# A cross network on one core: group 6's output gathered in a free input slot, group 7's output in group 6's slot, and group 6's last copy and store issued one tile sooner

## The chip, the cores and the metric

The kernel runs on one core of a Trainium2 chip. The metric is the device time of one execution in microseconds. A core has TensorE (matmul), VectorE, ScalarE, GpSimd and SyncE, which run their own instruction queues side by side and wait for each other through semaphores. In the profile they are PE, DVE, ACT, POOL and SP. DMAs are issued by instructions in such a queue (here nearly all by SP, in order) and carried out by 16 DMA engines.

## The reference

A cross network over 16,384 rows of 416 features, with six layers, in bfloat16:

```python
B, F, D, L = 16384, 26, 16, 6          # Din = 26 * 16 = 416
def reference(x0, ws, bs):             # x0 (B, Din), ws (L, Din, Din), bs (L, Din)
    x = x0
    L = ws.shape[0]
    for l in range(L):
        proj = jnp.einsum('bd,de->be', x, ws[l]) + bs[l]
        x = x0 * proj + x
    return x
```

## The kernel before

The rows are cut into eight groups of 2,048 (`GC`), numbered 0 to 7; `LAST` is 7. A group is four chunks of 512 rows (`NJ`, `CH`). Features lie on the partitions: 416 are three tiles of 128 (`NT`, tiles 0 to 2) and a tail of 32. A job (g, l) is layer l of group g. For each tile it multiplies on TensorE, ScalarE takes the result out of PSUM with the bias added (`evacuate`, L519, and `evacuate_chunk`, L555), and VectorE multiplies by x0 (L528, L567) and adds x (L533, L572). The tails of several jobs are done together (`tails`).

The input of a group is kept transposed in one of five slots `x0s[0]` to `x0s[4]`; `slot(g)` is g modulo 5. A slot is loaded by DMAs that transpose. Results of a layer lie in `xs`, tails in `x3s`.

The result of layer 5 lies with features on partitions and must be written row by row. For groups 0 to 6, `turn` (L888) issues one transposing DMA per tile into the tile `ost`, `turn_tail` (L896) one for the tail into `ot3`, `spread` copies the tail from `ot3` to its columns, and `store` (L929) writes the rows to DRAM. All these DMAs are issued by SP. There is one `ost` for groups 0 to 6, so the first `turn` of a group waits until the store of the group before has landed. `ost` also serves as a buffer while groups are loaded. For groups up to 5 `spread` is on GpSimd, for group 6 on ScalarE (L920).

Group 7's last layer is done the other way round: its matmuls (L1143) make rows on the partitions at once, in four steps `kk` of 128 rows of each chunk. ScalarE takes each out into the tile `on` (L1195), VectorE multiplies it by x0 (L1201) and adds the residual x (L1207), and `nat_store` (L1214) writes it. The residual has to be turned from features on partitions to rows: `rest_turn` (L941) does that with transposing DMAs for tiles 0 and 1 of job (7, 4) into `x5n`; tile 2 is turned on TensorE and copied by VectorE (L1163), the tail by TensorE and ScalarE (L1176).

`x0n7`, `x5n` and `on` lie in input slots that are free by then: slot 3, slot 0 and slot 4.

The end of the program runs so: stream of matmuls (L1051, L1055) up to job (7, 4) tile 0; then tiles 1 and 2 of job (7, 4); after tile 0 and after tile 1 `rest_turn` is added to SP's queue, after tile 2 ScalarE's `spread` and the two halves of group 6's store; then group 7's last layer. `turn` of group 6 is added to SP's queue as each tile of job (6, 5) is finished, its last tile in two halves.

Instructions are collected by a small class `Program`: `add` takes the engine, the tokens read and written, and works out what an instruction waits for. Each engine executes its instructions in the order in which they were added; on VectorE alone an addition can be held back behind the next multiply. A DMA's `lane` is the semaphore that it counts on; DMAs of one lane and different `batch` wait for the batch before.

Of the kernel before, what the change touches and what calls it, by code (L numbers as in the profile page):

```python
# [3 lines left out]
P = 128  # L4
CH = 512
# [16 lines left out]
class Program:  # L22
# [12 lines left out]
    def add(self, eng, fn, reads=(), writes=(), lane=None, batch=None, hold=False, release=False, row=None):  # L35
        op = Op(eng, fn, lane, batch, row)
        deps = {}
        if eng == "pool":
            writes = list(writes) + ["pool"]
        for t in reads:  # L40
            w = self.writer.get(t)
            if w is not None:
                deps[id(w)] = (w, True)
        for t in writes:
            w = self.writer.get(t)
            if w is not None:
                deps[id(w)] = (w, True)
            for r in self.readers.get(t, ()):
                if id(r) not in deps:
                    deps[id(r)] = (r, False)  # L50
        for d, raw in deps.values():
            if d.lane is None and d.eng == eng and lane is None and (eng == "pe" or not raw):
                if row is None or d.row is None or row == d.row:
                    continue
            op.deps.append(d)
        for t in reads:
            self.readers.setdefault(t, []).append(op)
        for t in writes:
            self.writer[t] = op
            self.readers[t] = []  # L60
        if eng == "dve":
            if hold:
                self.flush()
                self.held = op
            else:
                self.queue[eng].append(op)
                if release:
                    self.flush()
        else:
            self.queue[eng].append(op)  # L70
        if lane is not None:
            batches = self.lanes.setdefault(lane, [])
            if not batches or batches[-1][0] != batch:
                batches.append((batch, []))
            batches[-1][1].append(op)
        return op
# [233 lines left out]
def bass_standalone__cross_network_dcn__recsys_kernel(  # L310
# [6 lines left out]
    B, D = x0.shape  # L317
    L = ws.shape[0]
    NT = 3
    NJ = 4  # L320
    GC = NJ * CH
    NG = B // GC
    KK = CH // P
    assert D == NT * P + T32 and B == NG * GC and NG == 8 and L == 6
    LAST = NG - 1
# [18 lines left out]
    XW = NT * GC  # L344
# [7 lines left out]
    x0s = [nc.alloc_sbuf_tensor(f"x0_{s}", [P, XW + 2 * CH], BF16) for s in range(NX0)]  # L352
    xs = [nc.alloc_sbuf_tensor(f"x_{s}", [P, XW], BF16) for s in range(NXS)]
# [3 lines left out]
    ost = nc.alloc_sbuf_tensor("ost", [P, GC // P, D], BF16)  # L357
    Tb = ost[:, :, :].rearrange("p a f -> p (a f)")[:, 0:GC]
    ot3 = nc.alloc_sbuf_tensor("ot3", [P, KK, P], BF16)
# [8 lines left out]
    def x0_tok(s, t, j):  # L368
        return ("x0", s, t, j)

    def x0_all(s):
        return [x0_tok(s, t, j) for t in range(NT) for j in range(NJ)] + [("x03r", s), ("x03r", s, "b")]
# [4 lines left out]
    def slot(g):  # L377
        return g % NX0
# [56 lines left out]
    def x03_toks(s):  # L435
        return [("x03q", s, j) for j in range(NJ)]
# [303 lines left out]
    def load_nat(j, k0, k1):  # L740
# [6 lines left out]
        reads=["warm"], writes=["warm"])  # L747
# [117 lines left out]
    def job_banks():  # L865
        return take(NJ)

    view = "p (j k f) -> p j k f"
    sn, so, s5 = slot(3), slot(4), slot(5)
    x0n7, x5n, on = (x0s[s][:, 0:XW + CH].rearrange(view, j=NJ, k=KK) for s in (sn, s5, so))  # L870
    rows7 = x0[LAST * GC:B, :]

    def load_last():
# [9 lines left out]
    def turn(g, t):  # L883

        s = xset[(g, L)]
        halves = ((0, 2), (2, NJ)) if (g, t) == (LAST - 1, NT - 1) else ((0, NJ),)
        for j0, j1 in halves:
            add("sp", lambda h, j0=j0, j1=j1: h.dma_start_transpose(  # L888
                ost[:, j0 * KK:j1 * KK, t * P:(t + 1) * P], xs[s][:, t * GC + j0 * CH:t * GC + j1 * CH]),
                reads=[("x", s, t, j) for j in range(j0, j1)], writes=[("ost", t, j) for j in range(j0, j1)],  # L890
                lane="ot" if g < LAST - 1 else f"ot_{t}{j0}", batch=g)

    def turn_tail(g):

        s3 = xtail[(g, L)]
        add("sp", lambda h: h.dma_start_transpose(ot3[:, :, :], x3s[s3][:, :]),  # L896
            reads=[("x3", s3)], writes=["ot3"], lane="ot3", batch=g)

    def output(g):

        s, s3 = xset[(g, L)], xtail[(g, L)]
        if g < LAST - 2:
            turn(g, 0)
        if g < LAST - 1:
            turn_tail(g)
            spread("pool")
            if g < LAST - 2:
                turn(g, 1)
                turn(g, 2)
            store(g, 0, NJ)  # L910
        free_x.append(s)
        free_3.append(s3)

    def spread(eng):

        dst = ost[:, :, NT * P:D].rearrange("p (j k) f -> p j k f", j=NJ)
        sp_ = ot3[:, :, :].rearrange("p k (j f) -> p j k f", j=NJ)
        kw = dict(reads=["ot3"], writes=[("ost", NT, j) for j in range(NJ)])
        if eng == "act":
            add("act", lambda h: h.activation(dst, sp_, ACT_F.Copy), **kw)  # L920
        else:
            add(eng, lambda h: h.tensor_copy(dst, sp_), **kw)  # L922

    def store(g, j0, j1):

        rows = out[g * GC + j0 * CH:g * GC + j1 * CH, :]
        o = ost[:, j0 * KK:j1 * KK, :].rearrange("p (j k) f -> p j k f", k=KK)
        pat = "(j p k) f -> p j k f" if g == 0 else "(j k p) f -> p j k f"
        add("sp", lambda h: h.dma_start(rows.rearrange(pat, j=j1 - j0, k=KK), o),  # L929
            reads=[("ost", t, j) for t in range(NT + 1) for j in range(j0, j1)],  # L930
            writes=[("out", g, j0)], lane="out", batch=g)

    x5f = x0s[s5][:, 0:XW + CH].rearrange("p (a f) -> p a f", f=D)
# [1 line left out]
    def rest_turn(t):  # L935

        s = xset[(LAST, L - 1)]
        if t == 0:
            add("pool", lambda h: h.memset(warm[:, :], 0.0), writes=x0_all(s5) + x03_toks(s5) + ["x5 free"])
        for j0, j1 in ((0, NJ),) if t == 0 else ((0, 2), (2, NJ)):  # L940
            add("sp", lambda h, j0=j0, j1=j1: h.dma_start_transpose(  # L941
                x5f[:, j0 * KK:j1 * KK, t * P:(t + 1) * P], xs[s][:, t * GC + j0 * CH:t * GC + j1 * CH]),
                reads=[("x", s, t, j) for j in range(j0, j1)] + ["x5 free"],
                writes=[("x5n", j, t) for j in range(j0, j1)], lane=f"x5_{t}{j0}", batch=0)
# [15 lines left out]
    k = 0  # L960
# [17 lines left out]
    def start_job(g, l, ahead=True):  # L978
        started.add((g, l))
        if ahead:  # L980
            xset[(g, l + 1)] = free_x.pop(0)
        if (g, l) in W_LOAD:
            load_wm(W_LOAD[(g, l)], "sp")
            load_w3(W_LOAD[(g, l)], "sp")
        if (g, l) in G_LOAD:
            load_group(G_LOAD[(g, l)])
# [102 lines left out]
    for n, it in enumerate(items):  # L1089
        if n == s_lo:  # L1090
            stream(items[s_lo:s_hi], NJ, 0)
        if s_lo <= n < s_hi - 1:
            continue
        if it[0] == "tails":
            tails(it[1])
            continue
        _, (g, l), i = it
        if (g, l) not in started:
            start_job(g, l)
        if n == 0:  # L1100
            two_tiles(g, l)
            continue
        if n == 1:
            continue
        if n == s_hi - 1:
            pass
        elif mode[n] in ("FR", "F1"):
            banks = job_banks()
            full(g, l, i, banks, True, False, columns=items[n - 1][0] == "tails")
            rows32(g, l, i, banks, False, mode[n] == "F1")  # L1110
            evacuate(g, l, i, banks, list(range(NJ)), 2)
        else:
            banks = job_banks()
            rows32(g, l, i, banks, True)
            if n == len(items) - 1:
                full(g, l, i, banks, False, True, lambda j: evacuate(g, l, i, banks, [j], 1))
            else:
                full(g, l, i, banks, False, False)
                evacuate(g, l, i, banks, list(range(NJ)), 2)
        finish_tile(g, l)  # L1120
        if (g, l) == (LAST, L - 2) and i < NT - 1:
            rest_turn(i)
        elif (g, l) == (LAST, L - 2):
            spread("act")
            store(LAST - 1, 0, 2)
            store(LAST - 1, 2, NJ)


    g, l = LAST, L - 1
# [160 lines left out]
```

## Time and profile before

| | us |
|---|---|
| median of three runs | 468.71 |
| lowest and highest | 468.31, 469.32 |
| the profiled execution: its own time | 469.46 |
| the profiled execution: its span | 467.7 |
| busy: TensorE / VectorE / ScalarE | 458.6 / 403.9 / 379.4 |
| mean granted clock of TensorE | 0.997 |

The span runs from the first to the last event of the profiled execution; the execution's own time is some 2 us longer. Start times below are microseconds from the start of the span. A line of a timeline gives the start, the length, the engine, the line of the program, the operation, the tiles written and read, and how many instructions were merged into it. For a DMA issued by SP (SPq) the length is that of the issue; the time from issue to landing stands in the list of DMA issues. "x" as a tile name stands for `xs`, `x0s` and `x3s` alike, since numbers are left out.

### The profile page before, as it was taken

To read this page: it belongs to the slowest core of one execution; us is meant where nothing else is said; L and a number is where in the kernel's file an instruction comes from. 1 tells how busy PE (TensorE), PEld (TensorE's weight loads), DVE (VectorE), ACT (ScalarE), POOL (GpSimd) and SP (SyncE) were. 2 spreads that over 40 slices of the span, in tenths; PEclk is the share of its full clock that TensorE was granted. 3 is DMA by queue.
4 is the path that set the end of the run, shared out by engine and by line. 5 is a ranking of instruction groups with operands and counts; after the bars stand their busy time and mean duration, and the time that the engine had idled before them with its cause. 6 is when DMAs were issued, how large, how long until landed. Compare 5 with 4: busy or idle time off the path is not lost.

```text
span 467.7 us, 17583 instructions
## 1 busy us (share of the span) xinstructions
PE 458.6 (98%) x7888; PEld 266.7 (57%) x7893; DVE 403.9 (86%) x700; ACT 379.4 (81%) x609; POOL 8.8 (2%) x15
## 2 busy tenths in 40 slices
PE   9999999999999999999999999999999999999994
PEld 5344567665566565665646555565556656555441
DVE  2887989888898989898989898988989899889986
ACT  4587887888888797888878888788888888887883
POOL 1000000000000000000000000100000000001000
PEclk9999999999999999999999999999999999999998
DMA  7976870651001997097919457990100095701799
GB/s 214 193 141 152 142 141 24 114 104 26 2 25 14 174 232 119 19 143 185 176 32 162 127 110 114 154 313 5 25 4 25 13 167 153 120 21 40 192 186 294
DMA packets 139087, 53.77 MB, mean 115 GB/s; under 512 B 112762, under 2 KB 138500, under 8 KB 139012
## 3 DMA queue, kind: packets, MB, share of 16 engines
q1 hardware_dynamic: 138856, 52.54, 53.7%
q8 instruction: 61, 1.00, 0.9%
q10 hardware_dynamic: 156, 0.11, 0.1%
q14 instruction: 14, 0.11, 0.1%
HBM read 5.97 MB, written 13.63 MB: 42 GB/s over the span
## 4 chain that ended last, share of the span: by engine, by line
PE 90%; SPq 3%; DVE 3%; DMA 2%; issue 1%; ACT 1%; DVEq 0%; ACTq 0%
PE ps L1051 71%; PE ps L702 7%; PE ps L1055 6%; PE ps L655 4%; SPq L412 2%; PE ps L690 1%; DMA x<-in_x_dram 1%; DVE x L1207 1%; PE ps L643 1%; SPq L741 1%; DVE x L1201 1%; DMA x<-x 1%; ACT tw L519 1%; DVE x L533 1%; DVE tw L528 0%
## 5 line engine op out<-in xcount | busy, mean ns | idle before, releaser
L1051 PE MATMUL ps<-x,wm 32*128 32x512 bf16 x6144 | 364.4, 374 | 0.0
L555 ACT ACTIVATE tw<-ps,bias 128x512 bf16<-128x512 f32 x512 | 318.7, 688 | 49.6 <-PE ps L1051 36.5
L1051 PEld LDWEIGHTS ps<-x,wm 32*128 32x128 bf16 x6144 | 219.5, 92 | 129.1 <-ACT tw L555 3.8
L567 DVE TENSOR_TENSOR tw<-tw,x 128x1024 bf16<-128x1024 bf16 x256 | 171.9, 687 | 42.6 <-ACT tw L555 41.3
L572 DVE TENSOR_TENSOR x<-tw,x 128x1024 bf16<-128x1024 bf16 x256 | 167.1, 690 | 0.2
L1055 PE MATMUL ps<-x,w 32*128 32x512 bf16 x516 | 154.6, 374 | 0.0
L1055 PEld LDWEIGHTS ps<-x,w 32*128 32x128 bf16 x516 | 43.5, 92 | 6.6
L519 ACT ACTIVATE tw<-ps,bias 128x512 bf16<-128x512 f32 (+1 forms) x36 | 27.9, 861 | 9.3 <-PE ps L676 7.4
L702 PE MATMUL ps<-x,wm 128*32 128x512 bf16 x564 | 33.6, 380 | 0.0
L613 ACT ACTIVATE ts<-ps,bias 128x512 bf16<-128x512 f32 x32 | 20.4, 686 | 14.3 <-PE ps L690 14.3
L655 PE MATMUL ps<-x,wm 128*128 128x512 bf16 x123 | 28.4, 379 | 1.0 <-issue 0.6
L702 PEld LDWEIGHTS ps<-x,wm 128*32 128x32 bf16 x564 | 13.5, 96 | 18.7 <-issue 4.0
L655 PEld LDWEIGHTS ps<-x,wm 128*128 128x128 bf16 x128 | 11.7, 98 | 15.7 <-issue 2.8
L528 DVE TENSOR_TENSOR tw<-tw,x 128x1024 bf16<-128x1024 bf16 (+1 forms) x29 | 17.3, 613 | 2.9 <-ACT tw L519 2.8
L617 DVE TENSOR_TENSOR x<-ts,x 128x512 bf16<-128x512 bf16 x47 | 18.4, 418 | 0.3
L533 DVE TENSOR_TENSOR x<-tw,x 128x1024 bf16<-128x1024 bf16 (+1 forms) x29 | 16.7, 609 | 0.0
L922 POOL COPY ost<-ot 128x512 bf16<-128x512 bf16 x6 | 7.4, 1227 | 418.5 <-DMA ot<-x 418.5
L609 DVE SCALAR_TENSOR_TENSOR ts<-ps,bias,x 128x512 bf16<-128x512 f32 x15 | 11.2, 747 | 2.0 <-PE ps L690 2.0
L615 DVE TENSOR_TENSOR ts<-ts,x 128x512 bf16<-128x512 bf16 x32 | 12.8, 416 | 0.0
L1143 PE MATMUL ps<-wm,x 128*128 128x416 bf16 x48 | 9.8, 340 | 0.1
L1195 ACT ACTIVATE x<-ps 128x416 bf16<-128x416 f32 x16 | 7.6, 518 | 2.4 <-PE ps L1143 2.4
L806 DVE COPY x<-ps 128x512 bf16<-128x512 bf16 x5 | 2.0, 423 | 8.2 <-PE ps L796 8.2
(50 smaller groups left out, 70.9 us busy)
## 6 DMA issues: line engine op xcount, KB each, us to landing
out_dram<-ost SPq DMA_DIRECT2D x6, 1664.0 KB, 7.2
x<-x SPq DMA_DIRECT2D x24, 96.0 KB, 2.2
x<-in_x_dram SPq DMA_DIRECT2D x8, 208.0 KB, 4.1
x<-in_x_dram SPq DMA_DIRECT2D x4, 416.0 KB, 7.9
out_dram<-ost SPq DMA_DIRECT2D x2, 832.0 KB, 5.4
wm<-in_ws_dram SPq DMA_DIRECT2D x5, 312.0 KB, 3.4
x<-x SPq DMA_DIRECT2D x22, 64.0 KB, 2.0
out_dram<-x SPq DMA_DIRECT2D x3, 416.0 KB, 4.9
```

Of the source, the lines that this page charges most:

```text
L519: add("act", lambda h, a=a, w=w, b0=b0: h.activation(tw[r][:, a * CH:(a + w) * CH], psum[:, b0 * CH:(b0 + w) * CH], ACT_F.Identity, bias=b ...
L528: add("dve", lambda h, a=a, e=e: h.tensor_tensor(tw[r][:, a * CH:e * CH], tw[r][:, a * CH:e * CH], x0s[s0][:, i * GC + a * CH:i * GC + e * ...
L533: add("dve", lambda h, a=a, e=e: h.tensor_tensor(xs[so][:, i * GC + a * CH:i * GC + e * CH], tw[r][:, a * CH:e * CH], src(i, a, e), ALU.ad ...
L555: add("act", lambda h: h.activation(tw[r][:, j * CH:(j + 1) * CH], bank(b), ACT_F.Identity, bias=bias[:, i, l:l + 1], scale=1.0), reads=[( ...
L567: add("dve", lambda h: h.tensor_tensor(tw[r][:, o], tw[r][:, o], x0s[s0][:, c], ALU.mult), reads=[("tw", r, k) for k in both] + [x0_tok(s0 ...
L572: add("dve", lambda h: h.tensor_tensor(xs[so][:, c], tw[r][:, o], src(i, a, a + 2), ALU.add), reads=[("tw", r, k) for k in both] + [stok(i ...
L613: add("act", lambda h: h.activation(ts[r][:, :], bank(b), ACT_F.Identity, bias=bias[:, 3, l:l + 1], scale=1.0), reads=[("ps", b), "bias"], ...
L617: add("dve", lambda h: h.tensor_tensor(x3s[so][:, :], ts[r][:, :], res, ALU.add), reads=[("ts", r)] + rtok, writes=[("x3", so), ("x3", so, ...
L655: add("pe", lambda h, t=t, j=j, k=k, w=w: h.matmul(bank(banks[j])[:, k * w:(k + 1) * w], wm[l][:, t, ecols], src(t, j, j + 1)[:, k * w:(k ...
L702: add("pe", lambda h, t=t, j=j, src=src, l=l, b=b, ro=ro, qo=qo: h.matmul(psum[qo, b * CH:(b + 1) * CH], wm[l][:, t, NT * P:D], src(t, j, ...
L1051: add("pe", lambda h, l=l, t=t, j=j, b=b, q=q, ecols=ecols, src=src, kw=kw: h.matmul(bank(b), wm[l][q, t, ecols], src(t, j, j + 1)[q, :], ...
L1055: add("pe", lambda h, l=l, b=b, q=q, ecols=ecols, s3=s3, kw=kw: h.matmul(bank(b), w3[l][q, ecols], s3[q, :], **kw), reads=tok3 + [("w3", l ...
```

## The change

`on` moves from slot 4 to slot 6 modulo 5 = 1, which held group 6's input. Group 6's output is gathered in slot 4 (`ost6`) instead of `ost`. `out_tile(g)` gives the tile and its token. The first `turn` of group 6 takes the tokens of the slot's former content. The last `spread` and both halves of group 6's store are added one tile sooner: `spread` after tile 0 of job (7, 4) rather than after tile 2, the store after tile 0's `rest_turn`, and so ahead of tile 1's `rest_turn`.

```diff
-    sn, so, s5 = slot(3), slot(4), slot(5)
+    sn, s6, s5, so = slot(3), slot(4), slot(5), slot(6)
     x0n7, x5n, on = (x0s[s][:, 0:XW + CH].rearrange(view, j=NJ, k=KK) for s in (sn, s5, so))
+    ost6 = x0s[s6][:, 0:XW + CH].rearrange("p (a f) -> p a f", f=D)
+
+    def out_tile(g):
+        return (ost6, "ost6") if g == LAST - 1 else (ost, "ost")
...
     def turn(g, t):
 
         s = xset[(g, L)]
+        o, tok = out_tile(g)
+        free = x0_all(s6) + x03_toks(s6) if (g, t) == (LAST - 1, 0) else []
         halves = ((0, 2), (2, NJ)) if (g, t) == (LAST - 1, NT - 1) else ((0, NJ),)
         for j0, j1 in halves:
             add("sp", lambda h, j0=j0, j1=j1: h.dma_start_transpose(
-                ost[:, j0 * KK:j1 * KK, t * P:(t + 1) * P], xs[s][:, t * GC + j0 * CH:t * GC + j1 * CH]),
-                reads=[("x", s, t, j) for j in range(j0, j1)], writes=[("ost", t, j) for j in range(j0, j1)],
+                o[:, j0 * KK:j1 * KK, t * P:(t + 1) * P], xs[s][:, t * GC + j0 * CH:t * GC + j1 * CH]),
+                reads=[("x", s, t, j) for j in range(j0, j1)],
+                writes=free + [(tok, t, j) for j in range(j0, j1)],
                 lane="ot" if g < LAST - 1 else f"ot_{t}{j0}", batch=g)
...
-            spread("pool")
+            spread(g, "pool")
...
-    def spread(eng):
-
-        dst = ost[:, :, NT * P:D].rearrange("p (j k) f -> p j k f", j=NJ)
+    def spread(g, eng):
+
+        o, tok = out_tile(g)
+        dst = o[:, :, NT * P:D].rearrange("p (j k) f -> p j k f", j=NJ)
         sp_ = ot3[:, :, :].rearrange("p k (j f) -> p j k f", j=NJ)
-        kw = dict(reads=["ot3"], writes=[("ost", NT, j) for j in range(NJ)])
+        kw = dict(reads=["ot3"], writes=[(tok, NT, j) for j in range(NJ)])
...
     def store(g, j0, j1):
 
         rows = out[g * GC + j0 * CH:g * GC + j1 * CH, :]
-        o = ost[:, j0 * KK:j1 * KK, :].rearrange("p (j k) f -> p j k f", k=KK)
+        o, tok = out_tile(g)
+        o = o[:, j0 * KK:j1 * KK, :].rearrange("p (j k) f -> p j k f", k=KK)
         pat = "(j p k) f -> p j k f" if g == 0 else "(j k p) f -> p j k f"
         add("sp", lambda h: h.dma_start(rows.rearrange(pat, j=j1 - j0, k=KK), o),
-            reads=[("ost", t, j) for t in range(NT + 1) for j in range(j0, j1)],
+            reads=[(tok, t, j) for t in range(NT + 1) for j in range(j0, j1)],
             writes=[("out", g, j0)], lane="out", batch=g)
...
         if (g, l) == (LAST, L - 2) and i < NT - 1:
+            if not i:
+                spread(LAST - 1, "act")
             rest_turn(i)
-        elif (g, l) == (LAST, L - 2):
-            spread("act")
-            store(LAST - 1, 0, 2)
-            store(LAST - 1, 2, NJ)
+            if not i:
+                store(LAST - 1, 0, 2)
+                store(LAST - 1, 2, NJ)
```

The number of instructions on every engine stays the same. TensorE's, GpSimd's and VectorE's order is unchanged.

## The prediction

> **What bounds the kernel now.** I read the page's busy shares first, then the chain of waits over the last 38 us, then the DMA-issue queue of SP and VectorE in order of time, then the DMA engines by stage. The page gives TensorE 98% of the span, but that is a mean over stages: its last matmul ends at 460.7 us, and seven more microseconds follow. What those consist of is in the chain of waits (start us, length us, what):
>
> ```profile
> 453.50 3.26 DMA x<-x
> 456.75 0.03 issue
> ...
> 456.85 0.59 DVE x L1207
> 457.44 0.51 DVE x L1201
> ...
> 463.71 0.29 DVE x L1207
> 464.00 0.28 DVEq L175
> ```
>
> The end hangs on a transposing DMA `x<-x` that lands at 456.75. It is the last half of tile 1 of the last group's residual (`rest_turn`, L941). VectorE starts the add that waits for it at 456.85 and then works without a gap until 464.28: 7.43 us. The last two stores go out at 464.0 and 464.3 and land 2.9 us later; the span ends at 467.7. So in this stage the moment at which that transpose lands sets the end, one for one.
>
> When it lands is decided on SP. Its queue in order of time (start us, length us, engine, line):
>
> ```profile
> 431.40 0.41 SPq L929 DMA_DIRECT2D out_dram<-ost  x1
> 439.70 3.07 SPq L888 DMA_TRANSPOSE ost<-x  x1
> 442.83 1.25 SPq L896 DMA_TRANSPOSE ot<-x  x1
> 444.13 5.18 SPq L888 DMA_TRANSPOSE ost<-x  x3
> 449.42 5.41 SPq L941 DMA_TRANSPOSE x<-x  x3
> 455.00 1.14 SPq L929 DMA_DIRECT2D out_dram<-ost  x2
> 457.47 6.91 SPq L1214 DMA_DIRECT2D out_dram<-x  x5
> ```
>
> I name the steps T0 (439.70), ot (442.83), T1, T2a, T2b (the three from 444.13), X0, X1a, X1b (the three from 449.42), then the two halves S of group 6's store at 455.00. From 439.70 on SP issues one transpose after the other with no gap above 0.06 us, and the DMA engines keep pace with it (stages in us; the last two columns are DMA share and GB/s):
>
> ```profile
> 448.00:456.00 8.00, 7.94 (x74) 3.92 (x72) 6.91 (x16) 6.50 (x15) 0.00 (x0) 1.00 1.03 192
> 457.00:461.00 4.00, 3.73 (x26) 1.60 (x24) 3.90 (x8) 3.36 (x8) 0.00 (x0) 1.00 1.08 337
> 461.00:465.00 4.00, 0.00 (x0) 0.00 (x0) 3.21 (x9) 0.28 (x1) 0.00 (x0) 0.99 1.11 332
> ```
>
> The 16 engines are full in all three stages: with transposes at 192 GB/s up to 456, with stores at 332 to 337 GB/s afterwards. The queue of DMA work is thus one line, and its order matters: X1b is served before S now.
>
> **The change, part by part.** First, T0 no longer shares a tile with the store of group 5. That store is issued at 431.40 and lands 8.2 us later, at 439.6; T0 starts 0.1 us behind it. The other thing that T0 needs is the last add on tile 0 of group 6, on VectorE:
>
> ```profile
> 437.92 0.69 DVE L572 TENSOR_TENSOR x<-tw,x 128x1024 bf16<-128x1024 bf16 x1
> ```
>
> It ends at 438.61, so T0 can go at 438.7: 1.0 us sooner. What follows has its data by then: ot needs the tail's add, which ends at 439.41; T1 an add that ends at 441.82; T2a and T2b 443.62 and 444.22; X0 446.63. Each is issued later than that even after a shift by 1.0, so the whole line moves by 1.0 us. Term: -1.0. T0 took 3.07 us to issue here, while two earlier ones (372.30, 399.95) took 1.95 and 1.98; with that, the line moves by 2.1. I take -1.0, since nothing in the change touches what made this one long, and keep -2.1 for the range.
>
> Second, the slot that takes T0 to T2 held group 4's input, last read long before; the slot that now takes the last group's output held group 6's input, whose last reader is a VectorE multiply that ends at 443.02. ScalarE first writes there at 452.10. Neither wait costs anything.
>
> Third, `spread` moves on ScalarE in front of eight evacuations (L519, tiles 1 and 2). It takes 0.67 us (449.67 now). In its new place ScalarE idles from 444.44 to 445.09, 0.65 us. It needs ot, which lands at 442.83 + 2.5 = 445.3 now and 444.3 after the shift. Cost 0.0 to 0.1. If ot were as late as before, the evacuations of tile 1 would be 0.9 us late; behind them stand TensorE's last matmuls (end 460.7) and VectorE, which waits for X1 anyway until after 459. So still nothing.
>
> Fourth, and this decides: SP issues S between X0 and X1a. X0's issue ends at 449.42 + 2.68 - 1.0 = 451.1. S then waits for spread (445.1), for T2a (lands at 450.0 now, 449.0 after), for group 5's store (439.6) and, the second half, for T2b (451.6 now, 450.6 after): all there, so S goes out at 451.1 and 451.6, about 3.9 us sooner than now. It costs SP 1.14 us, so X1a is issued at 452.3 against 452.14. But 1,664 KB, 1.704 MB, now stand in front of it, at 332 to 337 GB/s: 5.1 us. X1b lands at 456.75 - 1.0 + 5.1 = 460.85. Term: +5.1.
>
> That a transfer behind a store waits for it is shown for ordinary copies. The same 32 KB copy, alone at 423.53 and 1.8 us behind a group's store at 385.60 (KB, us to landing):
>
> ```profile
> x<-x SPq DMA_DIRECT2D x1, 32.0 KB, 1.8
> ```
>
> ```profile
> x<-x SPq DMA_DIRECT2D x1, 32.0 KB, 5.1
> ```
>
> The store there was issued at 383.78. Its 5.1 us of data, after the same first 1.0 to 1.2 us, end near 390; the copy lands at 390.7. For a transpose behind a store before has no row in this stage, so the bounds are 0 (it is not held) and 5.1 + 1.6 (below); I take the copies' answer, 5.1.
>
> [...]
>
> Fifth, what waits on VectorE. Its queue is in order: the first L1207 waits for X1a, the second for X1b, and behind them stand fourteen more multiplies and adds, on which all the last group's stores wait. TensorE and ScalarE don't wait for them. VectorE has both first multiplies done at 454.47, so it idles until X1b, starts at 460.95, and ends 7.43 us later, at 468.4, against 464.28. That is 4.1 = 5.1 - 1.0, nothing added.
>
> Sixth, the end. The last stores of 104 KB take 2.9 us now, with the engines still full. With S gone before, a residual step makes 416 KB (1.3 us of transfer) every 2.26 us, so the last ones meet idle engines. No store of that size stands alone in the trace; copies of 32 and 96 KB alone take 1.8 and 2.1 us. Bounds 1.8 and 2.9; I take 2.2, beside the copy of 96 KB. Term: -0.7.
>
> Sum: -1.0 + 5.1 - 0.7 = +3.4 us. The profiled execution took 469.46 us with a span of 467.7, so it would become 472.9 with a span of 471.1. It stands 0.75 above the median of the runs, 468.71; on the median the forecast is 472.1.
>
> **The rivals.** (A) Not slower: the transposes are not held up by the store, because the DMA engines hold them apart. Then X1b lands at 455.75, VectorE ends at 463.3, the last transfers too come 1.0 sooner: 467.7. It decides if X1b lands before 456.7. For it: transposes move only 192 GB/s where stores reach 335, so something other than the write rate limits them. Against it: both are issued by SP onto one queue (q1 in the page's list), and the copy above was held.
>
> (B) Shared service: store and transposes take turns. X0 to X1b land 3.0 us apart now (453.7 and 456.75), so with half the engines X1 needs 6.0 us from 452.7: X1b at 458.7, +1.95, less 0.7 at the end: 470.0. [...]
>
> (C) SP is held as well: X1a can only be issued when the store has drained. X0 lands at 452.7, S needs 5.1 us more: 457.8. Then X1b is issued 1.36 later and lands 3.3 after that, at 462.5, 1.6 later than forecast: 473.7. For it: copies behind the store at 383.78 took up to 1.36 us to issue instead of 0.6. Against it: six of them were issued before that store landed.
>
> (D) The change doesn't bring T0 forward, since something else holds it: the -1.0 is gone, 473.1.
>
> **How the numbers follow.** Chances: forecast 0.72, A 0.06, B 0.08, C 0.10, D 0.04. The forecast's own bounds are 472.1 - 1.1 (short T0) = 471.0 and 472.1 + 0.7 (no relief at the end) + 0.6 (two thirds of one stretched transpose: T1 landed 6.2 us after 376.02 where 4.3 to 4.6 is usual for its neighbours, 1.6 to 1.9 more) = 473.4. To hold 8 in 10 the range takes in C and reaches toward B: 470.2 to 473.8. A change under 0.2%, 0.94 us, can't be told from none here. A lies at -1.0, on that edge; B, C, D and the forecast lie above it: faster 0.05, same 0.03, slower 0.92.
>
> **What would show it.** In the changed profile: T0 issued near 438.7 and no longer behind the store's landing; S issued near 451 with X1a right behind it; X1b landing near 460.9, over 7 us after its issue where it took 3.3; VectorE idle for some 5 us and again 0.7 in front of the first two adds (L1207, in the new text L1217), where it idles 1.08 and 0.70 now; a last store that lands in near 2.2 us; and DMA engines with gaps after 461. I am wrong if X1b lands before 458, or if VectorE's work after it is not the 7.43 us of now.

## The result, and the profile after

The changed kernel takes 472.43 us (median of 4 runs, 471.70 to 472.82); the kernel before took 468.51 in the same comparison (4 runs, 467.79 to 469.32). The ratio is 1.0081, 95% interval 1.0059 to 1.0104: slower by 0.6 to 1.0%, 3.9 us between the medians. The profiled execution took 471.70 us with a span of 469.7.

SP's queue after the change (start us, length us, engine, line):

```profile
430.74 0.41 SPq L938 DMA_DIRECT2D out_dram<-ost  x1
438.58 2.04 SPq L894 DMA_TRANSPOSE x<-x  x1
440.67 1.71 SPq L903 DMA_TRANSPOSE ot<-x  x1
442.43 5.50 SPq L894 DMA_TRANSPOSE x<-x  x3
448.03 2.22 SPq L950 DMA_TRANSPOSE x<-x  x1
450.45 1.27 SPq L938 DMA_DIRECT2D out_dram<-x  x2
451.76 6.34 SPq L950 DMA_TRANSPOSE x<-x  x2
460.66 6.91 SPq L1224 DMA_DIRECT2D out_dram<-x  x5
```

With the names of the prediction: T0 at 438.58, ot, then T1, T2a and T2b, X0 at 448.03, the store S at 450.45, and X1a and X1b in the line of 6.34 us. Those two took 2.69 us to issue before; now SP stands in them that long, while the store's packets run from 451.72 to 457.09.

The chain of waits of the same execution (start us, length us, what):

```profile
455.77 4.17 DMA x<-x
459.95 0.03 issue
...
460.04 0.59 DVE x L1217
...
467.19 0.29 DVEq L175
```

X1b lands at 459.95 (456.75 before). VectorE starts at 460.04 and ends at 467.48, 7.44 us later, where it took 7.43 before. The idle time stands in VectorE's own order (in brackets: us idle before the instruction, and what ended it):

```profile
453.71 1.14 DVE L1211 TENSOR_TENSOR x<-x,x 128x832 bf16<-128x832 bf16 x2
459.17 0.59 DVE L1217 TENSOR_TENSOR x<-x,x 128x832 bf16<-128x832 bf16 x1 [4.33 <-DMA x<-x]
460.04 0.59 DVE L1217 TENSOR_TENSOR x<-x,x 128x832 bf16<-128x832 bf16 x1 [0.28 <-DMA x<-x]
```

The DMA engines by stage (the last two columns are DMA share and GB/s):

```profile
444.00:451.50 7.50, 7.01 (x46) 2.95 (x45) 6.85 (x15) 6.20 (x12) 0.00 (x0) 1.00 1.08 204
452.00:457.00 5.00, 5.00 (x48) 2.48 (x46) 2.84 (x6) 3.62 (x9) 0.00 (x0) 1.00 1.07 329
457.00:460.00 3.00, 3.00 (x24) 1.41 (x22) 0.59 (x1) 2.39 (x5) 0.00 (x0) 1.00 0.95 167
460.00:465.00 5.00, 1.10 (x7) 0.39 (x4) 4.82 (x9) 1.62 (x4) 0.00 (x0) 0.87 0.49 166
465.00:469.00 4.00, 0.00 (x0) 0.00 (x0) 2.44 (x8) 0.00 (x0) 0.00 (x0) 0.50 0.66 218
```

The reader sees the order on the queue: transposes at 204 GB/s, the store at 329 GB/s from 452 to 457, the last transposes from 457 to 460 at 167 GB/s, and then engines with a share of 0.49 and 0.66, since the stores left wait for VectorE. The same bytes move as before, but the wait for X1 and the last group's stores now come after the big store, not beside it. The last store therefore lands sooner (KB, us to landing; 2.9 before):

```profile
out_dram<-x ACTq DMA_DIRECT2D x1, 104.0 KB, 1.7
```

Between the two profiled spans lie only 2.0 us (467.7 and 469.7). The span of the kernel before is 466.9 us in the median over 29 runs made for the first group of experiments, 465.7 at the least; that of the changed kernel is 470.1 over its four runs. So the first profile of before was 0.8 us longer than usual, and 3.2 us is the difference of the median spans. The difference of 3.9 in the whole times is 0.7 us more: 0.3 of it lies outside the spans (2.3 us in the four runs of the changed kernel, 2.0 in those 29), and 0.4 between the medians of the kernel before in the two comparisons (468.51 here, 468.89 there).

### The profile page after: what moved, and what is told of

Read it like the earlier page. It is cut to its first block, busy times and chain, and to the rows that moved or that the text cites. A ratio compares the mean times of both kernels' runs of the same rounds, so it can differ in the third digit from the quotient of the medians.

```text
span 469.7 us, 17581 instructions
## 1 busy us (share of the span) xinstructions
PE 459.0 (98%) x7888; PEld 267.7 (57%) x7893; DVE 403.7 (86%) x700; ACT 379.0 (81%) x609; POOL 6.3 (1%) x15
## 4 chain that ended last, share of the span: by engine, by line
PE 92%; DVE 4%; DMA 2%; ACT 1%; issue 1%; SPq 0%; DVEq 0%
PE ps L1060 70%; PE ps L702 7%; PE ps L1064 6%; PE ps L655 4%; PE ps L643 1%; PE ps L690 1%; DVE x L1211 1%; DMA ot<-x 1%; DMA x<-x 1%; DVE x L1217 1%; PE ps L778 1%; PE ps L796 1%; PE ps L676 1%; DVE x L533 1%; DVE tw L528 0%
## 5 line engine op out<-in xcount | busy, mean ns | idle before, releaser
L533 DVE TENSOR_TENSOR x<-tw,x 128x1024 bf16<-128x1024 bf16 (+1 forms) x29 | 16.7, 610 | 0.0
L930 POOL COPY ost<-ot 128x512 bf16<-128x512 bf16 x6 | 4.8, 800 | 420.0 <-DMA ot<-x 420.0
L1153 PE MATMUL ps<-wm,x 128*128 128x416 bf16 x48 | 9.8, 340 | 0.5 <-DVE x L533 0.5
```

The costliest lines, as they stand in the source:

```text
L533: add("dve", lambda h, a=a, e=e: h.tensor_tensor(xs[so][:, i * GC + a * CH:i * GC + e * CH], tw[r][:, a * CH:e * CH], src(i, a, e), ALU.ad ...
```

## The experiments

### The store put back

The changed kernel with the store behind `rest_turn(1)`, the slots and the earlier spread kept:

```diff
             rest_turn(i)
-            if not i:
+            if i:
                 store(LAST - 1, 0, 2)
                 store(LAST - 1, 2, NJ)
```

> The changed kernel with only the two halves of group 6's store put back behind tile 1's residual transposes (X1); slots and the earlier spread stay. Theory Q (the loss is the place in the DMA queue): X1b lands near 455.7, VectorE ends near 463.3, the engines stay full to the end, so the last store again takes near 2.9 us; 1.0 us faster than before, about 467.5 us. Rival S (the loss comes from the earlier spread on ScalarE or from the other slots): the loss stays, about 472.4 us.

Measured: 468.50 us against 468.89 for the kernel before, ratio 0.9998 (0.9984 to 1.0013). The whole loss is gone. In its profile X1b landed at 455.57 and VectorE ended at 463.1, as expected; the last stores took 2.9 to 3.0 us again. The gain of 1.0 us that was expected of it did not come, though: 0.4 between the medians, and the interval of the ratio holds 1.

### The slots alone

The changed kernel with store and `spread` both back behind tile 2 of job (7, 4):

```diff
         if (g, l) == (LAST, L - 2) and i < NT - 1:
-            if not i:
-                spread(LAST - 1, "act")
             rest_turn(i)
-            if not i:
-                store(LAST - 1, 0, 2)
-                store(LAST - 1, 2, NJ)
+        elif (g, l) == (LAST, L - 2):
+            spread(LAST - 1, "act")
+            store(LAST - 1, 0, 2)
+            store(LAST - 1, 2, NJ)
```

> The two slots alone: spread and store stand where they stood before the change. Theory Q: as with the store alone put back, about 467.5 us, within 0.5 of it. Rival S, as far as it lies in the earlier spread: 0.5 us or more faster than the kernel with spread moved, since TensorE's last layer then starts without the wait of 0.5 us that the changed kernel shows in front of L1153.

Measured: 468.44 us, ratio 0.9989 (0.9978 to 1.0000). Within 0.1 of the kernel with spread moved, so the earlier spread on ScalarE costs nothing that can be seen. Again a gain of some 0.4 us, not 1.0.

### Half of the store ahead of X1

The changed kernel with only its second half behind `rest_turn(1)`:

```diff
             rest_turn(i)
             if not i:
                 store(LAST - 1, 0, 2)
+            else:
                 store(LAST - 1, 2, NJ)
```

> The changed kernel with only the first half of the store (832 KB) ahead of X1, the second behind it. Theory Q: the hold is bytes over rate, 0.852 MB at 335 GB/s = 2.5 us instead of 5.1, so X1b lands near 458.3, VectorE ends near 465.8, the last store lands in 1.7 to 2.9 us: 0.4 to 1.6 us slower than before, about 469.5 us. Rival F (any store in front stops the transposes by a fixed time, whatever its size): as the changed kernel, about 472.4 us.

Measured: 469.92 us, ratio 1.0020 (1.0008 to 1.0033), 1.0 us above before. Its chain of waits:

```profile
453.85 4.25 DMA x<-x
458.11 0.03 issue
```

To see the hold by itself, take the time from X0's landing to X1b's, between which nothing else is to be served when the store is behind: 453.72 to 456.75, 3.03 us, in the first profile of before, and 452.82 to 455.57, 2.75 us, with the store put back. With half the store between them it is 453.00 to 458.11, 5.11 us; with the whole store, in the changed kernel, 452.43 to 459.95, 7.52 us. Beside the 2.75, the half adds 2.4 us and the whole 4.8: by bytes, not by a fixed time. Rival F falls.

The records of single packets in the traces show the hold directly. The transposes' packets there are of 256 bytes, this store's of 832. In the changed kernel the transposes' packets stop from 451.90 to 456.74, 4.85 us, while the store's run from 451.72 to 457.09; with half the store they stop for 2.32 us. Apart from 0.2 to 0.4 us at either end the two do not run side by side. All packets of the changed kernel from 452 to 456.7 us (the 16 under 512 B are of 4 bytes each):

```profile
DMA packets 1932, 1.59 MB, mean 339 GB/s; under 512 B 16, under 2 KB 1932, under 8 KB 1932
```

### The order alone

The kernel before with only the end of the loop changed, the output still gathered in `ost`:

```diff
         if (g, l) == (LAST, L - 2) and i < NT - 1:
+            if not i:
+                spread("act")
             rest_turn(i)
-        elif (g, l) == (LAST, L - 2):
-            spread("act")
-            store(LAST - 1, 0, 2)
-            store(LAST - 1, 2, NJ)
+            if not i:
+                store(LAST - 1, 0, 2)
+                store(LAST - 1, 2, NJ)
```

> The kernel before with spread and store one tile sooner and nothing else: output still gathered in ost, so T0 still waits for group 5's store. Theory Q with T0's term: 1.0 us slower than the changed kernel, about 473.4 us, T0 issued near 439.7. Rival N (bringing T0 forward is worth nothing since the transposes' engines are the limit and lose it again): the same as the changed kernel, about 472.4 us.

Measured: 473.04 us, ratio 1.0087 (1.0069 to 1.0105). In its profile T0 is issued at 439.64, 0.1 us behind the store of group 5 (issued at 431.43, landed after 8.1), and X1b lands at 461.69. The time lies 0.6 us above the changed kernel's 472.43, between what theory Q with T0's term (473.4) and rival N (472.4) gave; the two were timed in different comparisons and their intervals overlap, so by itself this settles only that the order makes the loss without the slots.

### Where T0's microsecond went

Two ideas remained. C: TensorE's instructions are fetched in blocks of 16 KB by the same DMA engines (the page of before lists q8 instruction with 61 packets, 1.00 MB and 0.9% of the 16 engines), and such a block falls into T0 to T2 and stops them. W: the wait that was removed binds only in some executions. The kernel before was profiled a second time, unchanged, and three kernels got 84 instructions more on TensorE ahead of the stream, which was to move the blocks:

```diff
-    HALVES = ((1, 2), (2, 1), (3, 0))
+    HALVES = ((0, 0),)
...
-    def keep_busy(n, b):
+    def keep_busy(n, b, w=4):
...
-            m = min(n, 4)
+            m = min(n, w)
...
-    keep_busy(25, 7)
+    keep_busy(25, 7, 1)
```

> The kernel before, unchanged, for a second profile of it. If the first profile (span 467.7 us) was a slow one, as the spans of 465.7 to 467.8 of its other runs say, X1b lands 0.5 to 1.0 sooner than 456.75 here and the span is near 467.0. If it was typical, X1b lands at 456.75 again.

> The two slots alone, and TensorE's program longer by 84 instructions ahead of the stream: the 25 warm-up blocks as 25 matmuls rather than 7 and 24 matmuls of the first job (with their weight loads) cut into two halves of 256 columns; nothing else. Theory C (T0 brought forward is worth only 0.4 us because TensorE's instruction block of 16 KB, fetched on the same DMA engines at 442, stops T0 for 1.5 us): 84 instructions at some 38 per us put that block near 438, before T0; then no stretch of low GB/s at 442 to 444, T0 lands near 443, X1b near 454.5, 1.0 to 1.6 us faster than the slots alone, about 467.2 us. Rival D (the transposes' own rate, or the reading of the same tiles, makes the gap): the gap stays where it is and the time stays at 468.4 us, or rises by what the longer start costs.

> The kernel before with the same 84 instructions more. Theory C: the block comes before T0 (439.7), T0 is issued in 2.0 us rather than 3.07, X1b lands near 455.7: up to 1.0 us faster than before, about 468.0 us, and 0.6 to 1.0 slower than the slots with the same shift. Rival D: no change, 468.9 us.

> The changed kernel with the same 84 instructions more. Theory C: T0 to X0 lose the gap, the store goes out 1.0 to 1.5 us sooner and X1b lands near 458.6: about 471.0 us, still slower than before by 2. Rival D: 472.4 us.

The second profile of before has a span of 466.4, and speaks for W. Group 5's store, SP's next instruction, and the add that T0 needs:

```profile
430.60 0.41 SPq L929 DMA_DIRECT2D out_dram<-ost  x1
438.44 1.70 SPq L888 DMA_TRANSPOSE ost<-x  x1
```

```profile
437.73 0.69 DVE L572 TENSOR_TENSOR x<-tw,x 128x1024 bf16<-128x1024 bf16 x1
```

The store landed 7.0 us after its issue, at 437.6, not after 8.2 as in the first profile. The add ends at 438.42, and T0 goes 0.02 us later. So T0 did not wait for the store at all in this execution: here the changed slots would have brought it nothing. X1b landed at 455.38, 1.4 sooner than in the first profile, with nothing changed.

What makes the store land late can be read from the two profiles. From 435.5 to 439.5 us, in 40 slices, the first and then the second (a block counts with all its 16 KB in the slice in which it starts):

```profile
GB/s 324 358 349 316 324 333 349 300 333 316 324 316 333 308 341 324 488 266 125 33 17 17 17 0 0 8 8 8 8 8 8 17 25 25 25 8 0 82 0 0
...
q8 instruction: 1, 0.02, 1.5%
```

```profile
GB/s 358 300 349 300 341 300 349 291 349 258 142 33 42 33 197 0 0 0 0 0 0 0 0 0 0 0 0 0 0 0 0 0 0 0 0 82 0 0 0 0
...
q8 instruction: 1, 0.02, 1.5%
```

In the first, the block (437.14 to 438.10 by the packet records) comes while the store is running, and after it the store's last packets come at 8 to 25 GB/s for another 1.0 us. From 438.15 to 439.10 only 1.1 packets are in flight on average, where it is 12.9 from 431 to 437; and one sixteenth of the 337 GB/s of the stores is 21. So this looks like one engine of the 16 that ended late. That it had to fetch the block first is the author's estimate from the order in time; no record names the engine. In the second, the store's last packet ends at 437.02, just after the block's start at 436.98, and nothing is left to be held up. All thirteen profiles of this case divide in this way: in the four in which the store landed after 7.0 us its last packet ended before the nearby block was over, in the nine with 7.9 to 8.5 us a block had come and gone between the store's issue and its last packet. That is a reading of profiles; no run was made to try it by itself.

The slots can save only what the store lands behind the add. In four of the thirteen profiles that is nothing, in the other nine 0.1 to 1.0 us, and 0.4 us in the mean of all.

The kernels with 84 instructions more: slots alone 469.14 us (ratio 1.0015, 1.0003 to 1.0027), before 469.23 (1.0012, 1.0001 to 1.0023), changed kernel 472.22 (1.0082, 1.0068 to 1.0096). No gain; the first two became slower. The shift did what it was to do to the gap, however. From 440.5 to 444 us, in 40 slices, the profile of the slots alone without the shift (second one, below) and with it:

```profile
GB/s 217 217 219 217 225 205 217 184 237 222 377 190 184 182 111 56 12 0 0 0 0 9 6 9 9 12 9 9 9 15 212 284 293 290 298 194 205 281 284 260
...
q8 instruction: 1, 0.02, 1.7%
```

```profile
GB/s 222 208 214 211 225 214 222 211 222 225 205 219 211 217 199 184 222 182 182 234 234 222 217 225 214 132 33 0 0 0 0 0 0 64 187 225 222 208 228 196
```

In the first, one instruction block is among the packets (441.40 to 442.37), and when it is over the transposes trickle at 6 to 15 GB/s for 0.8 us; in the second there is no block and no trickle, only a pause of some 0.5 us. X1b lands at 454.80 in the first and at 454.79 in the second, but T0 was issued 0.33 us later in the second, so the block did cost time. Over all thirteen profiles, X0 is issued 8.99 to 9.13 us after T0 in the four in which the block is over by 440.1 (the three kernels with 84 instructions more, and that with 60 below), and 9.45 to 10.04 us in the nine in which it starts between 440.0 and 442.3. T0's 3.07 us of issue in the first profile belong here too: its block starts at 440.58, and T0 takes 3.36 us in the order alone (440.84) and 3.06 with 36 instructions more (440.02), but 1.7 to 2.5 in the ten other profiles.

With the shift a further block comes at the end. From 452 to 468 in the slots alone with the shift:

```profile
GB/s 195 144 205 210 195 292 343 318 316 341 329 323 343 329 329 335 335 318 341 327 329 333 331 337 316 341 337 318 327 331 214 35 21 21 2 0 0 0 0 0
...
q8 instruction: 1, 0.02, 0.4%
...
out_dram<-x ACTq DMA_DIRECT2D x1, 104.0 KB, 3.9
```

The stores run at 316 to 343 GB/s up to 464, and then 1.6 us at 35 to 2 GB/s, as if one engine of the 16 ended late, and the last store takes 3.9 us instead of the 2.9 of the slots alone. In the kernel before with the shift X1b landed at 456.81 although T0 had been issued in 2.03 us: the further block, at 454.77 to 455.70, met X1b, which landed 5.2 us after its issue instead of 3.3. In the changed kernel with the shift it came at 457.17 to 458.04, and X1b landed at 460.77, 0.8 later than without, though T0 had gone at 438.05. A second, smaller pair of shifts, by 36 (the warm-up blocks alone) and by 60 instructions (12 matmuls of the first job cut in two besides), was to move the first block without bringing the second, beside the slots alone on the same chip:

> The two slots alone with 36 instructions more ahead of the stream (the 25 warm-up blocks as 25 matmuls). Theory C: the block asked for at about 440 moves to about 439.2, ahead of T0's data at 439.7 to 440.2, and no further block is asked for before 456: T0 to X1b run without a gap, X1b near 454.5, VectorE done near 462.1, about 467.3 us. If a further block shows up between 450 and 460 as with 84 instructions, or if the block still meets T0, no gain: 468.4 us.

> The same with 60 instructions more (12 matmuls of the first job cut in two besides). Theory C: the block comes at about 438.6, clear of T0; if no further block shows up before 456, 467.3 us; if it does, as with 84 instructions, 469.1 us.

> The two slots alone, again, on the same chip as the two above. Theory W (T0's wait for group 5's store binds only in executions where that store lands late, so the slots are worth 0 to 0.4 us): 0.0 to 0.4 us faster than before, about 468.4 us, with T0 issued right behind tile 0's add whatever the store does. Rival (worth 1.0 us as forecast): 467.6 us.

Measured: 468.80 us with 36 (ratio 0.9998, 0.9989 to 1.0007), 469.06 with 60 (1.0009, 1.0000 to 1.0018), 468.08 for the slots alone (0.9991, 0.9983 to 1.0000). With 36 and with 60 a block again lay among the last stores, and the strips have the same slow tail: from X1b's landing to the end of the span it takes 12.1 and 12.0 us, with 84 instructions 11.9, in the slots alone 11.0. With 36 the first block still met T0. With 60 it did not, and X1b landed 16.4 us after T0's issue instead of 16.7 and 17.1 in the slots alone; the end took more than that back, and 469.06 is what theory C gave for that case (469.1).

So C holds this far: by the 9.45 to 10.04 us from T0 to X0 with a block among them and the 8.99 to 9.13 without, it costs some 0.3 to 1.1 us there. But it is not the place of the missing microsecond. Both profiles of before and both of the slots alone have such a block, and from T0's issue to X1b's landing take 17.1 and 16.9 us before, 17.1 and 16.7 with the slots: what T0 gains is not lost behind it. It was not there to gain in every execution, as W says. The slots alone gain 0.4 and 0.7 us in two comparisons, beside the 0.4 us that the thirteen profiles give; 0.7 is more than the 0.0 to 0.4 expected of W and less than the rival's 1.0. They are the best of the versions tried, ahead of both kernels by the median, though both intervals end at 1.0000.

## Why the prediction was right

The forecast was 472.1 us and slower; 472.43 was measured. Its steps one by one:

- The order on the queue: right, and the whole of the loss, as the store put back and the order alone show. The hold was mis-sized a little: 5.1 us were forecast from bytes over rate, 4.8 us lie between X0's landing and X1b's beyond the 2.75 with the store put back. (SP's queue had one gap of 0.10 us, in front of X0, where the prediction saw none above 0.06; nothing hung on it.)
- T0 brought forward by 1.0 us: this term was wrong in size. It was read from one profiled execution in which group 5's store landed late. That it was 0.75 us above the median of the runs was noted in the prediction, but the term was not lowered for it. The slots alone are worth 0.4 to 0.7. In the changed kernel's profile T0 did go at 438.58, 0.02 us behind its add, but so it did at 438.44 in the second profile of before.
- The end: 0.7 us of relief were forecast, from a landing of 2.2 us; the last store lands in 1.7 us, and from VectorE's end to the end of the span it takes 2.2 us instead of 3.4. This term measured 1.2.
- With the measured sizes (the gain of T0 as about 0.5) the sum is -0.5 + 4.8 - 1.2 = +3.1, beside 3.2 between the median spans. That the forecast of +3.4 came so near is in part luck, since the errors offset each other: the gain of T0 was 0.5 too large, the relief at the end 0.5 too small, the hold 0.3 too large. The 3.9 us between the two medians of whole times are 0.5 above the forecast.
- VectorE's work after X1b: 7.43 forecast, 7.44 measured. Nothing else on TensorE or ScalarE came onto the path. Its idle time in front of the first two adds was forecast as some 5 and 0.7 us and is 4.33 and 0.28.
- Spread on ScalarE: it cost more than the 0.0 to 0.1 of the forecast in its place. In the changed kernel's profile ot lands at 444.9, not 444.3, spread starts at 444.95, and TensorE stands 0.49 us in front of L1153. The cover that was named held: VectorE waited for X1 until 459.17, and with the store put back moving spread or not made no difference of more than 0.1 us.
- Rival C (SP held as well): half right. SP was held, 6.34 us in two issues, so that X1b was issued only at 455.77 and landed 4.2 us later, not over 7 as the forecast had it. But X1b landed at 459.95, not 462.5: the transposes' packets went on at 456.74, before the store's last one ended at 457.09, and SP's next store was not due before 460.66. Rivals A and B would have had X1b at 455.75 and 458.7; both fall with it, with the half store, and with the 4.85 us in which no packet of a transpose moved. Rival D (T0 is not brought forward) falls against the first profile of before, where T0 went at 439.70; against the second, with 438.44, it would be right.

## What to carry to other kernels

With the DMA engines full here (share 1.07 to 1.08 in the changed kernel), moving a store up in the queue moved X1b behind it back by about the store's bytes over the rate: 2.4 us for 832 KB and 4.8 us for 1,664 KB, at 329 to 339 GB/s. Where a profile shows engines as full, ask which consumer of the transfers behind it sets the end, before asking which transfer can go sooner. A wait read in one profiled execution has a size in that execution only: T0 went 1.1 us behind its add in the first profile of before and 0.02 us behind it in the second. When the two releasers of a wait lie within a microsecond of each other, as here, look at a second profile or at the spread of the spans, and take a part of it. And the store that went ahead of the end left a shorter last transfer here, 1.7 us instead of 2.9, so the end needs a term of its own.

## What was not expected of the hardware

Instructions are listed as packets among the DMA engines' work: q8 instruction on the page of before, 61 packets, 1.00 MB, each a block of 16 KB. With 84 more TensorE instructions the block that the slots alone show at 441.40 is not found between 440.5 and 444. A block takes 0.9 to 1.8 us by its packet record, in most cases about 1.0. Where one met transposes in flight, these stopped and then went on at 6 to 15 GB/s for 0.8 us instead of over 200 (440.5 to 444 above). T0 landed 5.7 us after its issue in the changed kernel, with a block at 441.88 to 442.81; in the slots alone with the shift, with none there, the median of T0, T1 and T2a is 4.3 us. Where a block lay among the last stores, the last of them landed 1.0 us later (3.9 us after its issue, not 2.9). A change of 36 to 84 instructions, 400 us earlier, moved the blocks of these kernels, and with it the 0.4 to 0.7 us that the slots alone had gained were gone (468.80, 469.06 and 469.14 us).

The same store of 1,664 KB, issued at the same place of the program, landed after 7.0 us in four profiles and after 7.9 to 8.5 in nine, and in the nine alone a block had come and gone before its last packet. By this reading the wait that the change removed hung on where an instruction block fell; that was seen in thirteen profiles, not tried by itself.
